# A transformer block on one core: another order of all its steps

## The chip, the cores and the metric

The kernel runs on one core of a Trainium2 chip. The core has TensorE (PE, with its weight loads shown apart as PEld), VectorE (DVE), ScalarE (ACT), GpSimd (POOL) and SyncE (SP), which here does nothing but issue transfers. Each engine takes its instructions from a queue of its own and in that queue's order; between queues, semaphores say when the data of one instruction are there for another. The metric is the device time of one execution in microseconds (us). Lower is better.

## The reference

2048 tokens of width 512 pass a normalized sliding-window attention (32 heads of 16, a window of 256) and a normalized gated feed-forward layer of width 1376, each with its input added:

```
q, k, v = qkv of layernorm(x) @ wqkv                 # 32 heads of 16
scores = einsum("bhqd,bhkd->bhqk", q, k) * (Dh ** -0.5)
mask = (idx[:, None] - idx[None, :] >= 0) & (idx[:, None] - idx[None, :] < W)   # W = 256
p = _softmax(where(mask, scores, -1e9))
h = x + (p @ v, heads put together) @ wo
g = layernorm(h) @ w_gate;  u = layernorm(h) @ w_up
out = h + (_sigmoid(g) * u) @ w_down
```

All inputs and the output are float32.

## The kernel before

**Numbers.** Every float32 product is made of float16 ones. A matrix is scaled by a power of two and split into a high half and a low half (a cast or copy, L355 and L357, then a subtraction, L362), and a product is three matmuls, high by high, high by low and low by high (L402 in `mm3`, also L1140 and L1317).

**Stage one, attention.** The tokens lie in 16 row tiles of 128, two to a block of 256 queries (8 blocks). For a block the steps are: load x (`load_x`, L473), layer norm (`normal`, L556 to L573: statistics on DVE, the root on POOL, the normalization), split, transposition on PE (L609) or by a transfer (L616); q and k (`do_qk`, L402, low half L661), v (`do_v`); keys and queries restacked through transfers (`do_keys`, L670 to L677, into `SK`; `do_queries`, L686, into `SQ`). `SK` has room for five half blocks, so a load into it waits until the scores that read its old content are done. Scores are computed twice: `do_s` (PE L740) for the row maxima, which DVE takes with the mask added (L725); `do_m` turns the maxima into two more rows of `SQ` (transposed by a transfer, L752, L756); `do_st` computes the transposed scores (L794 to L805), ACT their exponentials (L770), POOL cuts off what is masked (L778, L783). `do_pv` multiplies with v (L831), `do_o` transposes by a transfer and adds the halves into `OS` (L854, L861), and `do_wo` divides by the sums (L873, L875), splits, transposes, multiplies with wo (L402) and adds x (L899), which `load_again` (L480) has fetched a second time. Ahead of everything `prep` finds the largest element of wq, wk, wv and wo (L367 on ACT or L369 on DVE, the pieces together in L531), makes a scale of it (PE L380, DVE L384 to L388) and splits the weights (L537, L539).

Beside it, the weights of stage two are prepared: `do_amax` loads each piece of w_gate, w_up and w_down (L926) for its largest element (L369), `do_split` and `do_weights` load the pieces again and make scaled halves of them and of their sums.

**Stage two, feed-forward.** The row tiles go in 8 pairs, the columns in 3 cuts (512, 512, 352). `do_ln2` normalizes, splits and transposes a pair; `do_pair` makes the products of gate and up together with seven matmul groups where eight would be usual (a 2 x 2 scheme of Strassen's kind, L1140). Each group writes a PSUM bank; the result is copied out (`copied`, by L355 on ACT, by L357 or L359 on DVE) or added to what is there (`added`, L1161, L1163). A later group that adds onto the same bank waits for the copy. Then come sigmoid (ACT L1206), the product with up (DVE L1210), sums for the same scheme (L1224), halves, and a transposition by a transfer (`row`, L1240); `do_down` multiplies with w_down (L1317, L1323), adds into the rows (`taken`, `high`, L1288, L1300) and stores them (L1294).

**What sets the order.** Every step is a generator that stops once for each piece of work and says on which engines this piece may run. A table, `ORDER`, holds 4663 numbers, one for each piece of work, in the order in which all of them are recorded. `Planner.run` does no planning; it walks the table:

```
for code in ORDER:
    self.now = self.roots[code >> 7]
    item = self.now[code >> 2 & 31]
    costs, needs, *more = item[1]
    self.on = next(iter(costs)) if len(costs) == 1 else ENGINES[1 + (code & 3)]
```

The upper bits name the step (or the family of steps under one root), the middle bits the one of that family, and the last two bits the engine, DVE, ACT, POOL or DMA, where a piece can run on several. Since the program is recorded as it stands (`tc.manual_schedule`), the table fixes the order in each engine's queue and in SP's queue of transfers; waits come from the data and from the buffers' rings.

Of the kernel before, what the change touches and what calls it, by code (L numbers as in the profile page):

```python
# [61 lines left out]
    3203, 3331, 771, 899, 1027, 1155, 7424, 2179, 2435, 7808, 7426, 1411, 7424, 641, 2051, 7810, 7424, 641, 1539, 7424, 1667, 7808, 641, 7427, 7808,  # L62
    3459, 7810, 1795, 641, 2307, 6658, 640, 7424, 3587, 643, 7811, 640, 2691, 3075, 641, 7808, 2947, 640, 641, 2819, 640, 641, 8323, 640, 641, 8323,
    640, 8323, 1280, 1281, 1921, 8323, 1921, 3715, 8195, 1281, 1280, 1920, 8323, 13056, 1921, 8323, 8323, 8323, 1280, 12672, 13058, 1283, 8321, 8195,
    8195, 1280, 8195, 3843, 12674, 8195, 2561, 8195, 1920, 7042, 8320, 8195, 8195, 1281, 1923, 8193, 1280, 8451, 2561, 2560, 8192, 1281, 1280, 1281,
    8579, 9219, 1280, 1281, 2561, 3971, 8451, 9219, 1280, 8451, 8835, 12672, 8579, 6018, 1920, 8835, 12673, 8451, 13056, 9219, 1921, 8451, 12672,
    8451, 4099, 1921, 8451, 18304, 8451, 8963, 8579, 1922, 8449, 8579, 8963, 2560, 8579, 1921, 8448, 8579, 8835, 6274, 8579, 1921, 13056, 8579, 8963,
    17920, 12675, 13058, 8577, 2563, 12673, 8576, 17922, 1920, 1921, 8707, 13059, 18306, 7683, 8707, 1920, 13057, 1920, 7683, 1921, 8067, 1920, 8067,
    1920, 7683, 17920, 49667, 8067, 23168, 17921, 4227, 8067, 17920, 8707, 7683, 50691, 8064, 7681, 51075, 2560, 9091, 17923, 18304, 13443, 8707,
    2561, 13443, 23552, 13443, 2561, 13443, 17921, 13443, 18304, 4355, 23554, 13443, 18304, 13443, 6402, 9091, 13443, 28416, 13571, 13441, 13571,  # L70
    6530, 9091, 13571, 10371, 10371, 13571, 10372, 10376, 6786, 13571, 13440, 13571, 13571, 13571, 10371, 10371, 10371, 13569, 10384, 23170, 13699,
    10388, 13699, 50688, 2562, 13699, 10380, 49665, 13699, 13568, 13699, 13699, 13699, 13699, 23168, 10371, 10371, 14467, 10371, 13697, 13827, 10392,
    10400, 13827, 4483, 9347, 10396, 13827, 9348, 14211, 13827, 13696, 9347, 9347, 9347, 13827, 14083, 9352, 13827, 9360, 10883, 14211, 9356, 13827,
    10884, 13827, 28800, 14211, 18307, 13825, 10883, 9347, 10883, 18305, 9364, 10888, 13824, 9347, 10883, 2561, 9368, 18691, 13955, 10892, 33664,
    18691, 2561, 14083, 9347, 18691, 23169, 18691, 14467, 9372, 9347, 18691, 10896, 23170, 13955, 18819, 9376, 9603, 18691, 14467, 9604, 10883, 10883,
    9603, 10900, 18691, 10904, 51203, 9608, 18691, 23552, 10883, 9603, 9603, 18689, 18819, 10908, 4611, 9616, 18819, 10883, 9612, 18819, 10912, 18819,
    18688, 18819, 18819, 13955, 9603, 9603, 18819, 9603, 50435, 2560, 2561, 18817, 18947, 51331, 18947, 9620, 9624, 14339, 18947, 9628, 51073, 18947,
    18816, 14083, 9603, 18947, 2561, 18947, 14339, 18947, 2562, 18947, 50179, 9632, 11139, 10115, 19075, 18945, 10116, 10115, 11140, 19075, 10120,
    13955, 2561, 6146, 11139, 11139, 19075, 11144, 11148, 19075, 2561, 18944, 11139, 7170, 10115, 19075, 10115, 11152, 19075, 10128, 19075, 14339,
    10124, 11139, 12931, 11156, 34048, 28418, 11139, 10115, 10115, 19075, 12931, 19073, 10136, 11160, 12931, 10132, 51201, 19072, 11139, 11139, 10115,  # L80
    12931, 11164, 11168, 10140, 10115, 13315, 12929, 10144, 50433, 12416, 11651, 11651, 11651, 13315, 11652, 11656, 12419, 11660, 11651, 13315, 11664,
    11907, 11907, 13315, 11908, 11912, 0, 11651, 11651, 11651, 18563, 13313, 11668, 11672, 12419, 11676, 51329, 11651, 11907, 11907, 11680, 23171,
    11916, 18563, 49411, 11920, 23169, 23552, 19203, 11907, 11907, 11907, 18563, 11928, 23554, 19203, 11924, 11932, 11907, 16387, 16387, 11936, 9475,
    9475, 18563, 33666, 16388, 9477, 9481, 16392, 16387, 28802, 16387, 18561, 9475, 16396, 16387, 9475, 6914, 9485, 12544, 16387, 9489, 23555, 16400,
    12547, 16404, 9475, 23553, 16387, 18179, 16408, 28416, 16387, 9497, 15619, 16412, 9475, 4739, 18179, 16416, 50177, 50051, 15620, 15619, 9731,
    24195, 9501, 12547, 15624, 15619, 15619, 24195, 9733, 15628, 28417, 15619, 9731, 15632, 9731, 24195, 19203, 9741, 15636, 15619, 24195, 9737,
    15640, 15619, 15619, 9731, 15644, 9731, 9745, 24195, 15648, 9753, 15363, 9750, 9731, 15364, 15363, 24195, 9757, 19331, 9506, 15368, 10243, 16899,
    15363, 24195, 10245, 16900, 9494, 10243, 10243, 15372, 9859, 16899, 10249, 16899, 9762, 24195, 10253, 38912, 50049, 15363, 10243, 28418, 10243,
    9859, 10257, 16908, 10265, 16904, 7298, 49409, 15376, 16899, 28800, 10243, 15363, 16912, 16899, 10269, 10499, 4867, 18179, 15380, 50819, 9857,
    16916, 10499, 10274, 15363, 18179, 19331, 10501, 15384, 10505, 9856, 10499, 15363, 18177, 16899, 14851, 10499, 15388, 10509, 24323, 28419, 10513,  # L90
    16920, 10499, 14852, 10518, 15363, 10499, 10521, 16899, 15392, 24323, 10262, 50563, 16924, 10525, 14851, 16899, 24323, 14856, 19331, 50817, 14851,
    11011, 16928, 10530, 24323, 19459, 11013, 14851, 14860, 24323, 39296, 11011, 10627, 14851, 19459, 11011, 14851, 10627, 11021, 28801, 49795, 14872,
    19459, 11017, 14864, 28802, 24193, 14868, 11011, 9987, 11011, 11025, 14851, 24192, 24323, 11033, 2562, 11011, 14876, 14851, 14595, 11037, 28803,
    11267, 14880, 24323, 14595, 11030, 14596, 11269, 11267, 14595, 10625, 14600, 11267, 24323, 34050, 11273, 14604, 14595, 14595, 11277, 11042, 14608,
# [184 lines left out]
    61571, 62116, 61571, 62112, 62119, 61571, 61584, 61872, 61571, 62120, 62124, 60955, 61571, 62132, 61571, 62128, 61883, 62136, 61571, 62136, 61588,  # L279
    61571, 60315, 61571, 62139, 61571, 61571, 61592, 61888, 62211, 61888, 61884, 62211, 61891, 62211, 62211, 62212, 61884, 62211, 62140, 62211, 61887,  # L280
    62211, 62216, 62144, 62211, 62140, 62144, 62211, 62143, 62211, 62220, 62211, 61595, 62211, 62147, 62211, 62211, 62211, 59671, 62211, 60311, 62211,
    61591, 62224, 62211, 62211, 62211, 62211, 62228, 62211, 62231, 62211, 62211, 62211, 62232, 62235,
]

class Port(float):
# [1214 lines left out]
```

## Time and profile before

| | |
|---|---|
| median of 3 runs | 771.59 us (770.92 to 772.53) |
| the profiled execution | 770.99 us |
| its span on the core | 769.3 us |
| its mean granted TensorE clock | 0.989 |
| instructions | 19057 |
| transfers in the span | 118.57 MB, 154 GB/s |

A row of a timeline reads: start, duration, engine, source line, operation, result and source with their shapes, and in square brackets how long the engine had been idle and what ended that. `SPq` is SP's queue; its duration is that of issuing. `A <- B` among the waits means that an instruction of A's line waited and that B ended the wait. In a row of busy times "(x66)" is the number of instructions.

### The profile page before, as it was taken

The numbers are of one execution on the slowest core, as the hardware profiler recorded it, in microseconds if no ns is written. First come the engines' busy times: TensorE is split into PE (matmuls) and PEld (weight loads), VectorE is DVE, ScalarE is ACT, GpSimd is POOL, SyncE is SP. The second block draws the span as 40 slices with busy tenths as digits, with TensorE's granted clock in tenths as the row PEclk, the third lists the DMA queues.
The fourth block names the chain that finished last, engine by engine and source line by source line (L and its number), as shares of the span: only waits on it lengthen the run. The fifth ranks groups of instructions, "written<-read, shape, count | busy, mean of one in ns | idle before, by whom it ended". The sixth has DMA issues, their size and how long they took to land.

```text
span 769.3 us, 19057 instructions
## 1 busy us (share of the span) xinstructions
PE 729.6 (95%) x7030; PEld 502.0 (65%) x7030; DVE 692.9 (90%) x2067; ACT 436.9 (57%) x774; POOL 256.7 (33%) x319
## 2 busy tenths in 40 slices
PE   4899999999999999999999898699999999999997
PEld 3586678777686687686666554367565666666476
DVE  8999999978899999999998579999998989989973
ACT  5755788878688888798877667653222111121210
POOL 3333445535545466554757442240000000000000
PEclk9999999999999999999999999899999999999999
DMA  8586593886747989569587879455375665736535
GB/s 300 156 221 168 142 180 80 152 198 144 165 95 172 205 211 182 166 156 245 150 162 180 211 187 274 117 119 105 79 136 95 117 131 106 150 66 109 96 83 155
DMA packets 210318, 118.57 MB, mean 154 GB/s; under 512 B 174576, under 2 KB 183792, under 8 KB 210224
## 3 DMA queue, kind: packets, MB, share of 16 engines
q1 hardware_dynamic: 210224, 117.35, 67.9%
q8 instruction: 55, 0.90, 0.5%
q14 instruction: 39, 0.32, 0.2%
HBM read 43.65 MB, written 19.40 MB: 82 GB/s over the span
## 4 chain that ended last, share of the span: by engine, by line
PE 75%; DVE 11%; DMA 5%; issue 5%; ACT 3%; SPq 0%; DVEq 0%; ACTq 0%
PE mmp L402 18%; PE sp L1140 14%; PE mmp L1317 11%; PE pvp L831 7%; PE sp L740 6%; PE stp L1140 6%; PE pvp L1140 3%; PE stp L805 2%; PE stp L795 2%; DVE junk L725 2%; PE stp L794 1%; PE mmp L1323 1%; PE stp L796 1%; DMA oT<-whl 1%; ACT pa L770 1%
## 5 line engine op out<-in xcount | busy, mean ns | idle before, releaser
L725 DVE CUSTOM_DVE_ANT_0 junk<-sp,mask 128x320 uint8<-128x320 f32 (+4 forms) x512 | 215.4, 465 | 16.6 <-PE sp L740 14.0
L770 ACT ACTIVATE pa<-stp,kappa 128x512 f32<-128x512 f32 (+1 forms) x256 | 157.3, 645 | 48.0 <-PE stp L796 44.5
L1140 PEld LDWEIGHTS <-x 128*128 128x128 f16 x1008 | 98.3, 98 | 94.6 <-issue 10.1
L740 PE MATMUL sp<-SK,SQ 96*128 96x256 f16 (+3 forms) x960 | 129.6, 233 | 6.3 <-DVE mq L725 3.1
L402 PE MATMUL mmp<-xT,W 128*128 128x256 f16 x768 | 114.3, 281 | 3.3 <-DVE sq L661 1.7
L740 PEld LDWEIGHTS <-SQ 96*128 96x128 f16 x960 | 80.5, 97 | 30.9 <-issue 12.8
L1140 PE MATMUL sp<-W,x 128*128 128x512 f16 (+1 forms) x420 | 90.1, 351 | 6.5 <-ACT SQ L355 5.8
L770 ACT ACTIVATE pb<-stp,kappa 128x512 f32<-128x512 f32 x128 | 84.6, 685 | 19.7 <-PE stp L805 15.9
L402 PEld LDWEIGHTS <-W 128*128 128x128 f16 x768 | 71.4, 100 | 16.1 <-DVE W L539 2.9
L778 POOL TENSOR_SCALAR_AFFINE_SELECT pa<-pa 128x1024 f32<-128x1024 f32 x56 | 62.9, 1127 | 53.9 <-ACT pa L770 50.3
L831 PE MATMUL pvp<-pa,VT 128*17 128x128 f32 (+1 forms) x1408 | 62.5, 307 | 0.0
L795 PE MATMUL stp<-SQ,SK 100*128 100x256 f16 x224 | 60.2, 272 | 0.0
L563 POOL TENSOR_TENSOR rs<-rs,nhalf 128x1 f32<-128x1 f32 x32 | 20.2, 634 | 118.2 <-DVE rs L560 105.0
L783 POOL TENSOR_SCALAR_AFFINE_SELECT pa<-pa 128x512 f32<-128x512 f32 x64 | 42.6, 669 | 45.3 <-ACT pa L770 45.0
L1206 ACT ACTIVATE SQ<-sp,cg 128x512 f32<-128x512 f32 (+1 forms) x22 | 14.0, 636 | 76.6 <-PE sp L1140 76.3
L796 PE MATMUL stp<-SQ,SK 100*128 100x128 f16 x256 | 55.5, 219 | 0.7 <-ACT pb L770 0.4
L783 POOL TENSOR_SCALAR_AFFINE_SELECT pb<-pb 128x512 f32<-128x512 f32 x64 | 42.0, 658 | 42.6 <-ACT pb L770 40.1
L402 PE MATMUL mmp<-WO,oT 128*128 128x512 f16 x192 | 51.4, 389 | 2.5 <-DMA oT<-whl 2.5
L831 PEld LDWEIGHTS pvp<-pa,VT 128*17 128x17 f32 x1408 | 37.8, 97 | 22.7 <-issue 2.7
L362 DVE TENSOR_TENSOR SQ<-SQ,SQ 128x512 f16<-128x512 f32 (+3 forms) x93 | 50.2, 555 | 1.9 <-ACT SQ L355 1.3
L794 PE MATMUL stp<-SQ,SK 100*128 100x128 f16 x224 | 49.5, 221 | 1.3 <-DMA SQ<-mt 0.3
L805 PE MATMUL stp<-SQ,SK 100*128 100x256 f16 x256 | 48.1, 272 | 2.5 <-ACT pa L770 2.1
(226 smaller groups left out, 1445.8 us busy)
## 6 DMA issues: line engine op xcount, KB each, us to landing
SQ<-sq SPq DMA_DIRECT2D x96, 128.0 KB
wr<-chunk SPq DMA_DIRECT2D x28, 256.0 KB
SK<-mem SPq DMA_DIRECT2D x16, 384.0 KB
chunk<-in_wd_dram SPq DMA_DIRECT2D x20, 256.0 KB
X<-in_x_dram SPq DMA_DIRECT2D x16, 256.0 KB
mem<-sk SPq DMA_DIRECT2D x8, 512.0 KB
out_dram<-X SPq DMA_DIRECT2D x16, 256.0 KB
W<-wr SPq DMA_DIRECT2D x7, 512.0 KB
```

The lines of the kernel that those rows point to most:

```text
L402: PE.matmul(ps, a_of(a, k), b_of(b, k), start=(k == 0 and i == 0), stop=(k == n - 1 and i == 2))
L725: V.tensor_tensor_reduce(out=junk[:, c0:], in0=ps[:, c0:], in1=mask[:, c0:], scale=1.0, scalar=-3.0e38, op0=ALU.add, op1=ALU.max, accum_ou ...
L740: PE.matmul(ps[:, col:col + k1 - k0], q, SK[0:96, (2 * a + hf) % 5, 4 * (p % 2) + j, k0:k1], start=True, stop=True)
L770: S.activation(dst, a, AF.Exp, scale=kappa)
L778: G.affine_select(out=f, in_=f, pattern=[[0, 8], [-1, 128]], compare_op=ALU.is_gt, fill=0.0, base=0, channel_multiplier=1)
L783: G.affine_select(out=p, in_=p, pattern=[[0, 4], [1, 128]], compare_op=ALU.is_ge, fill=0.0, base=0, channel_multiplier=-1)
L795: PE.matmul(a[:, 128:384], ks(k0 + 1, g, j), qs(b, g, j, 0, 256), start=True, stop=True)
L796: PE.matmul(a[:, 384:512], ks(k0 + 3, g, j), qs(b, g, j, 128, 256), start=True, stop=True)
L805: PE.matmul(a[:, u, :], ks(k0 + 2, g, j + u), qs(b, g, j + u, 0, 256), start=True, stop=True)
L831: PE.matmul(ps[32 * j:32 * j + 17, u, q0:q1], VT[:, kt % 6, 8 * j + g, :], w[:, j, c:c + q1 - q0], start=first, stop=last, skip_group_chec ...
L1140: PE.matmul(ps, X2[p % 2][part][:, (a * COUNT[part] + at) * 2 + k, :], operand(c, j)[:, b, k, :], start=first and k == 0 and i == 0, stop= ...
L1317: PE.matmul(ps, hT[p, c, r][:, a, half * kinds[c] + i, :], W["d"][2 * c + i][:, b, j, :], start=fresh and c == 0 and i == 0 and n == 0, st ...
```

## The change

Only the table `ORDER` differs. Both tables have the same 4663 pieces of work. 109 of them run on another engine than before (57 leave DVE for ACT or POOL, 52 come to DVE), and the rest stand at other places. The start of the difference:

```
 ORDER = [
-    3203, 3331, 771, 899, 1027, 1155, 7424, 2179, 2435, 7808, 7426, 1411, 7424, 641, 2051, 7810, 7424, 641, 1539, 7424, 1667, 7808, 641, 7427, 7808,
...
+    3331, 899, 3203, 771, 1027, 1155, 7808, 3587, 2179, 7424, 2691, 2051, 7426, 641, 1539, 7810, 7424, 641, 2435, 7424, 7424, 641, 1795, 7808, 7427,
...
```

The first place is SP's queue at the start of the program, from its first transfer on; `X` holds the row tiles of x, `wq`, `wk`, `wv` and `OS` receive pieces of the weights:

```order
-L473 DMA X<-in_x_dram 128x512 x2
-L487 DMA wq<-in_wqkv_dram 128x512 x4
-L487 DMA wv<-in_wqkv_dram 128x512 x2
+L473 DMA X<-in_x_dram 128x512
+L487 DMA wq<-in_wqkv_dram 128x512
+L473 DMA X<-in_x_dram 128x512
+L487 DMA wq<-in_wqkv_dram 128x512 x3
+L473 DMA X<-in_x_dram 128x512
+L487 DMA wv<-in_wqkv_dram 128x512
+L487 DMA OS<-in_wo_dram 128x512
+L487 DMA wv<-in_wqkv_dram 128x512
```

Before, row tiles 0 and 1 came first and then the four pieces of wq. Now tile 1 comes first (3331), then a piece of wq (899), then tile 0 (3203), and the other three pieces; on DVE the statistics of tile 1 accordingly precede those of tile 0, while tile 0 is still normalized first.

The second place is SP's queue around the load of `SK` with the first half of block 4's keys. In the old order, from the transposition of a block's attention output (`oT<-whl`) to that load:

```order
L616 DMA_TRANSPOSE oT<-whl 128x8x128
L686 DMA SQ_73<-sq_102 32x2048 x2
L926 DMA chunk<-in_wd_dram 128x512
L756 DMA SQ_79<-mt 2x32x64 x2
L686 DMA SQ_73<-sq_102 32x2048
L926 DMA chunk<-in_wu_dram 128x512
L686 DMA SQ_73<-sq_102 32x2048
L926 DMA chunk<-in_wd_dram 128x512
L677 DMA SK<-mem 96x2048
```

In the new order:

```order
L616 DMA_TRANSPOSE oT<-whl 128x8x128
L854 DMA_TRANSPOSE RT<-RH 128x8x128
L686 DMA SQ_73<-sq_102 32x2048 x2
L926 DMA chunk<-in_wu_dram 128x512
L926 DMA chunk<-in_wd_dram 128x512
L677 DMA SK<-mem 96x2048
```

Two query loads and the maxima's transfer (L756) now stand ahead of the transposition, one of the loads of w_down pieces (L926) stands behind the keys, and a load of x by L480, which came after them, stands 31 places further ahead.

The third place is DVE's queue in stage two, at the last cut of pair 2 (`SQ<-sp` and `SQ<-stp` of 352 columns are copies of PSUM products). In the old order both copies were ACT's, and DVE had:

```order
L1288 SCALAR_TENSOR_TENSOR X<-mmp,cd,X 128x512
L1210 TENSOR_TENSOR SQ_73<-SQ_73 128x352
L1288 SCALAR_TENSOR_TENSOR X<-mmp,cd,X 128x512
L556 BN_STATS st_9054<-X 128x6
L558 BN_AGGR mv<-st_9054 128x2
L560 TENSOR_SCALAR rs<-mv 128x1
L1210 TENSOR_TENSOR SQ_73<-SQ_73 128x352
```

In the new order:

```order
L1288 SCALAR_TENSOR_TENSOR X<-mmp,cd,X 128x512
L1163 SCALAR_TENSOR_TENSOR SQ_73<-stp,SQ_73 128x352
L1210 TENSOR_TENSOR SQ_73<-SQ_73 128x352 x2
L357 COPY SQ_73<-sp 128x352
L357 CAST SQ_79<-SQ_73 128x352
L359 TENSOR_SCALAR SQ_73<-stp 128x352
L556 BN_STATS st_9070<-X 128x6
```

The two copies came to DVE, behind both multiplications of L1210 and ahead of the statistics of the next pair.

Elsewhere: in the attention stage between 160 and 417 us of the profile before, 22 pieces of work leave DVE and 17 come to it. Of the steps that leave, 5 are additions into `OS` (L861), 4 maxima (L369), 4 low halves (L362), 4 casts (L357), 3 copies of PSUM results and 2 sums of a pair (L1122); those that come are 6 additions, 2 maxima, 2 low halves, 4 casts, a PSUM copy and 2 multiplications of L875. In stage two 6 copies of PSUM products (`copied`) go from ACT to DVE and 5 the other way (with 2 more at 421 and 445 us, still in attention). At the end, the halves of the last transposed rows (L357, L362) stand ahead of two additions on DVE (L1288, L1300) that came before them, and on SP two stores (L1294) in place of one stand ahead of the last transposition (L1240).

442 rows, old and new, of the table ORDER are left out of this document.

## The prediction

> **What bounds the kernel now.** I read the page's totals and its chain first, then TensorE's waits, then busy times by stage.
>
> ```profile
> PE 729.6 (95%) x7030; PEld 502.0 (65%) x7030; DVE 692.9 (90%) x2067; ACT 436.9 (57%) x774; POOL 256.7 (33%) x319
> PE 75%; DVE 11%; DMA 5%; issue 5%; ACT 3%; SPq 0%; DVEq 0%; ACTq 0%
> ```
>
> TensorE is busy for 729.6 of 769.3 us and carries three quarters of the chain. A new order removes no matmul, so it can only win idle time of TensorE, 39.7 us, and stretches where a "busy" TensorE is fed slowly. VectorE, at 90%, is the second limit. TensorE's waits name what ended its idle time (columns: us in total, times, the longest):
>
> ```profile
> PE mmp L609 <- DVE RT L357: 7.0, 1, 7.0
> PE sp L1140 <- ACT SQ L355: 6.4, 2, 5.8
> PE sp L740 <- DVE mq L725: 3.1, 6, 1.2
> PE mmp L402 <- DMA oT<-whl: 2.5, 2, 2.1
> PE stp L805 <- ACT pa L770: 2.1, 2, 1.9
> PE sp L740 <- DMA SK<-mem: 1.6, 1, 1.6
> ```
>
> The reader is to see few, single waits: 7.0 before the first transposes, 5.8 once in the passage to the second stage, and 1.6 to 2.1 for a transfer here and there. Which stage lives under which limit, the windows tell (columns: stretch, its length, busy us of PE, PEld, DVE, ACT, POOL, granted clock, DMA share, GB/s):
>
> ```profile
> 200.00:220.00 20.00, 18.32 (x213) 14.02 (x210) 16.40 (x65) 13.74 (x22) 7.70 (x11) 0.91 0.62 144
> 400.00:420.00 20.00, 19.15 (x246) 12.74 (x245) 19.07 (x64) 14.58 (x25) 16.22 (x21) 1.00 0.79 192
> 480.00:500.00 20.00, 12.74 (x66) 6.85 (x65) 19.97 (x39) 13.25 (x26) 3.96 (x4) 0.83 0.50 113
> 520.00:740.00 220.00, 220.00 (x1428) 139.31 (x1426) 201.91 (x451) 45.92 (x83) 9.55 (x14) 1.00 0.57 108
> ```
>
> In attention (400 to 420) TensorE and VectorE are both near full. From 480 to 500 VectorE has no idle time and TensorE stands. From 520 to 740 TensorE has no idle time at all, so there the change can only lose.
>
> **The change, part by part.** The table holds the same 4663 steps, of which 109 change engine; TensorE's own order hardly moves. I go through the span and charge each part against the profiled execution's 770.99 us, its 769.3 of span and 1.7 around it. That execution is 0.6 below the median of the runs shown (771.59).
>
> *Start.* The first row tile of x is now loaded third, behind the second tile and a piece of wq. What hangs on it:
>
> ```profile
> 6.45 0.63 ACT L367 ACTIVATE W<-wq 128x512 f16<-128x512 f32 x1 [4.37 <-DMA wq<-in_wqkv_dram]
> 3.75 0.69 DVE L556 BATCH_NORM_STATS2 st<-X 128x6 f32<-128x512 f32 x1
> 4.77 0.68 DVE L556 BATCH_NORM_STATS2 st<-X 128x6 f32<-128x512 f32 x1
> 4.94 0.55 POOL L563 TENSOR_TENSOR rs<-rs,nhalf 128x1 f32<-128x1 f32 x1 [1.22 <-DVE rs L560]
> 5.91 0.54 DVE L573 TENSOR_SCALAR chunk<-X,mv,rs 128x512 f32<-128x512 f32 x1
> 8.13 0.43 DVE L357 CAST RT<-chunk 128x512 f16<-128x512 f32 x1
> 9.60 0.16 DVE L531 TENSOR_REDUCE am<-am 128x1 f32<-128x4 f32 x1 [1.05 <-ACT W L367]
> 12.38 0.61 PE L402 MATMUL mmp<-xT,W 128*128 128x256 f16 x2 [0.85 <-ACT W L537]
> ```
>
> ScalarE's first maximum waits for the third load, so the third place lands at 6.45; the first had landed by 3.75. From the statistics of the first tile to its root on POOL takes 5.49 - 3.75 = 1.74, and from the normalization (5.91) through split and second tile to the last cast 8.56 - 5.91 = 2.65. In the new order VectorE takes the second tile's statistics first, then the first's: 6.45 + 1.74 + 2.65 = 10.84. Behind stands the maximum of wq (L531), which came at 9.60 and was covered by 1.05 of idle time; it slips by 1.2. The scales, the weight pieces and the first matmul follow it without a gap, VectorE's queue stays full behind them, and nothing later catches up unless a stage has room. **+1.2**; ends: nothing, if x in third place lands as it did in second (statistics of the second tile started at 4.8 without a wait), and 1.3.
>
> *Keys of block 4, first half.* On SyncE's queue several loads stood ahead of the load of SK; one of them goes behind it, and a load of x goes far ahead.
>
> ```profile
> 198.58 2.21 SPq L926 DMA_DIRECT2D chunk<-in_wd_dram  x1
> 202.87 0.38 PE L805 MATMUL stp<-SQ,SK 100*128 100x256 f16 x2
> 204.49 6.62 DMA SK<-mem
> 211.16 0.47 PE L740 MATMUL sp<-SK,SQ 96*128 96x64 f16 x5 [1.58 <-DMA SK<-mem]
> ```
>
> The load overwrites keys that the scores of block 2 read last, which end at 202.87 + 0.38 = 203.25. It cannot be issued before that, so at most 204.49 - 203.25 = 1.2 of TensorE's 1.58 can be won, and something on the queue will take part of it: **-0.9** (0 to -1.6, the whole wait). The wait has a second price:
>
> ```profile
> 212.00:214.00 2.00, 2.00 (x16) 1.63 (x16) 1.99 (x9) 1.57 (x3) 0.00 (x0) 0.62 0.83 236
> 214.00:216.00 2.00, 2.00 (x16) 1.62 (x15) 1.00 (x4) 1.06 (x2) 0.00 (x0) 0.53 0.29 106
> 430.00:432.00 2.00, 0.47 (x3) 0.10 (x1) 0.70 (x2) 1.36 (x3) 0.00 (x0) 1.00 1.39 115
> ```
>
> Behind it TensorE's clock is 0.62 and 0.53 for two windows of 2 us: 0.38 x 2 + 0.47 x 2 = 1.7 us of matmul time lost, with VectorE idle for half of the second. A wait of 1.9 near 430 had no such sequel, so it doesn't come for certain; a shorter wait may escape it. I take half, **-0.8** (0 to -1.7). [...]
>
> *VectorE in attention, 160 to 417.* By the order, 22 steps leave VectorE for ScalarE or POOL there and 17 come to it. Their prices (columns: times; shortest, median, longest ns; first and last start):
>
> ```profile
> L861 DVE TENSOR_TENSOR OS<-RT x17: 429/436/869, 126.0 to 460.8; 128x272 f32<-128x272 f16 x17
> L369 DVE TENSOR_REDUCE amd<-chunk x7: 673/680/686, 196.1 to 247.2; 128x1 f32<-128x512 f32 x6, 96x1 f32<-96x512 f32 x1
> L362 DVE TENSOR_TENSOR whl<-OS,whl x9: 627/681/1218, 133.6 to 474.9; 128x512 f16<-128x512 f32 x9
> L357 DVE CAST whl<-OS x6: 415/420/806, 133.1 to 424.0; 128x512 f16<-128x512 f32 x6
> L875 DVE TENSOR_TENSOR OS<-OS,rc x7: 678/685/693, 132.4 to 463.7; 128x512 f32<-128x512 f32 x7
> L357 DVE COPY SQ<-sp x18: 515/681/693, 421.4 to 736.2; 128x512 f32<-128x512 f32 x13, 128x352 f32<-128x352 f32 x5
> ```
>
> Leaving: 5 adds (L861), 2 subtractions priced like them, 4 casts, and 4 maxima, 4 low halves and 3 PSUM copies at 0.68: 7 x 0.44 + 4 x 0.42 + 11 x 0.68 = 12.2. Coming: 6 adds, 4 casts, and 2 maxima, 2 low halves, 2 multiplies and 1 copy at 0.68: 6 x 0.44 + 4 x 0.42 + 7 x 0.68 = 9.1. Net 3.1 less. If TensorE were fed by VectorE alone, all of it would be won; if TensorE were the bound, nothing. In 400:420 both are within 1 us of full, so I take half: **-1.5** (0 to -3.1). What covers the steps that leave is ScalarE, 14.6 of 20, and POOL, 16.2 of 20.
>
> *Passage to the second stage, 420 to 505.* The waits on the transposes near 430 and 462 keep the same instructions ahead of them on ScalarE and SyncE: 0, though the first may now draw a slow clock, up to +1.7. In the VectorE-bound stretch up to 494, whose end releases TensorE's 5.8, two steps go and two come, each 0.4 to 0.7 by the rows above: **+0.2** (-0.6 to +0.6).
>
> *Feed-forward stage.* Six copies of PSUM products (L357, L359) go from ScalarE to VectorE, and five the other way. ScalarE had idle time; VectorE has a queue. One place, pair 2, last cut:
>
> ```profile
> 529.49 0.46 ACT L355 ACTIVATE SQ<-sp 128x352 f32<-128x352 f32 x1 [1.00 <-PE sp L1140]
> 529.12 0.74 DVE L1288 SCALAR_TENSOR_TENSOR X<-mmp,cd,X 128x512 f32<-128x512 f32 x1
> 530.78 0.52 DVE L1210 TENSOR_TENSOR SQ<-SQ 128x352 f32<-128x352 f32 x1
> 531.08 1.06 PE L1140 MATMUL sp<-W,x 128*128 128x352 f16 x6
> ```
>
> The copy ended at 529.95, and the product that adds onto the same bank starts at 531.08: 1.13 of room. Now the copy stands behind the add of L1288 and the multiply that came at 530.78: 529.86 + 0.52 + 0.51 (the shortest of its kind above) = 530.9, 0.2 in time. TensorE never waits as long as such margins hold. A loss at one or two of the six: **+0.5** (0 to +4.1, six times 0.68).
>
> *End.* TensorE waits 0.8 for the last transpose, which SyncE issues at 758.25, 11 us from the end. Its data are ready up to 1 us sooner, since two adds now stand behind them on VectorE, but two stores instead of one stand ahead of it on the queue:
>
> ```profile
> 757.59 0.57 SPq L1294 DMA_DIRECT2D out_dram<-X  x1
> 758.25 2.52 SPq L1240 DMA_TRANSPOSE RH<-SQ  x1
> 762.27 0.50 PE L1317 MATMUL mmp<-WD,RH 128*128 128x256 f16 x3 [0.81 <-DMA RH<-SQ]
> ```
>
> The second costs 0.6, so **-0.2** (0 to -0.8) is left.
>
> The sum is 1.2 - 0.9 - 0.8 - 1.5 + 0.2 + 0.5 - 0.2 = -1.5: 769.5 for the profiled execution, and 770.1 against the median.
>
> **The rivals.** *More of a gain.* x in third place lands early enough (by about 5.2) to leave the start as it is, and VectorE is the true bound through attention, so that all 3.1 arrive: 0 - 1.7 - 3.1 + 0.5 = -4.3, or 767.3. For it speaks VectorE's 19.07 of 20; against it, that TensorE shows only 3.1 us of waits for the row maxima (L725), and the landing at 6.45.
>
> *Slower, through the PSUM copies.* The mechanism is the one above: a copy that waits in VectorE's queue holds back the next product, in a stage where TensorE has no slack to give it back. It decides where VectorE's queue ahead of the copy exceeds the room (0.2 in the place worked out). If all six lose a copy's length, 4.1 stand in place of 0.5: 773.7, and 774 to 776 if one of the waits also slows the clock. For it: 201.91 of 220 busy on VectorE. Against it: the copies that went to ScalarE ease VectorE elsewhere, and the margin, though thin, is positive.
>
> *Nothing that counts.* TensorE's order is nearly the old one and its streams are full, so engines off its path may be shuffled without effect: 771.6.
>
> **How the numbers follow.** The forecast 770.1 has 0.45, the larger gain 0.20, the copies 0.28, no effect 0.07. What can be told from no change is about 0.2%, 1.5 us. The forecast's own range is 767.5 to 773; it lies on the edge of what can be told, so I give 0.22 of its chance to faster, 0.20 to the same and 0.03 to slower. With the others: faster 0.22 + 0.20 = 0.42, the same 0.20 + 0.07 = 0.27, slower 0.03 + 0.28 = 0.31. The range for 8 times in 10 reaches below the larger gain and past most of the copies' case: 766.0 to 775.5.
>
> **What would show it.** The start is right if L531 on VectorE starts near 10.8 and the first matmul of L402 moves from 12.4 to about 13.6. The keys' term is right if TensorE's wait for SK shrinks below 1 us and no window behind it has a clock near 0.6. The relief is right if VectorE is busy about 3 us less between 160 and 417 and the last row max of block 7 comes earlier by more than the start lost. The rival with the copies shows as waits of L1140 for L357 or L359 between 520 and 740, where TensorE has none now. The forecast is wrong if a new wait of over 1 us, with a slow clock behind it, stands anywhere between 160 and 505: one such costs up to 3.4 and eats the sum.

## The result and the profile after

The new order is slower: 776.13 us median (774.69 to 778.38, 7 runs) against 770.92 of the old order's runs beside it (766.17 to 772.53). The ratio is 1.0094, with a 95% interval of 1.0073 to 1.0116. That is under one per cent, and clear of the noise. A second set of runs of the same kernel gave 1.0095 (1.0075 to 1.0114). The forecast was 770.1, and its range ended at 775.5. The profiled execution took 777.85, its span 776.1.

The busy times of the page after (us, share of the span, instructions):

```profile
PE 731.5 (94%) x7030; PEld 503.2 (65%) x7030; DVE 695.1 (90%) x2061; ACT 438.9 (57%) x782; POOL 257.3 (33%) x322
```

VectorE was to lose 3 us of work in attention alone. It has six instructions fewer than before, yet is busy 2.2 us longer (692.9 before). Its instructions have become longer, not more. TensorE's waits after, the longest sums first:

```profile
PE mmp L609 <- DVE RT L357: 8.6, 1, 8.6
PE sp L1140 <- ACT SQ L355: 5.3, 2, 5.2
PE sp L740 <- DVE mq L725: 5.0, 6, 1.5
PE mmp L402 <- DVE sq L661: 3.2, 4, 1.8
...
PE mmp L402 <- ACT VT L355: 0.8, 2, 0.7
...
PE stp L1140 <- DVE SQ L359: 0.7, 1, 0.7
```

The wait for SK is gone; waits for VectorE's row maxima (3.1 before, 5.0 now) and others for VectorE have grown. Stretches of the same times as before, with 40 to 60 added (the work in them is not the same to the microsecond, since the new execution lags):

```profile
40.00:60.00 20.00, 17.08 (x162) 14.22 (x160) 18.55 (x78) 10.29 (x18) 9.05 (x13) 1.00 0.92 224
200.00:220.00 20.00, 19.51 (x274) 14.39 (x272) 18.89 (x70) 15.35 (x28) 8.84 (x12) 1.00 0.80 154
520.00:740.00 220.00, 218.80 (x1424) 138.83 (x1422) 204.81 (x461) 44.52 (x78) 15.39 (x20) 1.00 0.55 105
```

and 40 to 60 before:

```profile
40.00:60.00 20.00, 19.48 (x186) 16.65 (x184) 19.32 (x85) 11.53 (x20) 7.07 (x7) 1.00 0.84 215
```

There TensorE works 2.4 us less while POOL works 2.0 more. Taking each matmul after against the same matmul before, the median delay is 0.7 us for those at 20 to 40, 3.8 at 40 to 60 and 5.2 at 60 to 80. Most of the loss is there after 80 of 776 us. The delay falls to 3.2 at 80 to 100, where the old execution loses time of its own (at 76 and 88, see below), and is 4.9 at 100 to 120, 5.0 at 160 to 180, 2.7 at 220 to 240 (behind the old execution's wait for SK), 7.6 at 420 to 440, 7.8 at 600, and 6.8 at the end. What happens in the first part shows in the timeline of POOL and VectorE:

```profile
35.77 0.95 POOL L505 MEMSET SK<- 32x1024 f32 x1
35.95 1.05 DVE L573 TENSOR_SCALAR xn<-X,mv,rs 128x512 f32<-128x512 f32 x1
...
41.20 1.31 DVE L573 TENSOR_SCALAR xn<-X,mv,rs 128x512 f32<-128x512 f32 x1 [0.78 <-POOL rs L563]
41.28 0.95 POOL L505 MEMSET SK<- 32x1024 f32 x1
...
48.23 1.80 POOL L516 MEMSET SQ<- 32x2048 f32 x1
48.31 0.35 DVE L725 CUSTOM_DVE_ANT_0 junk<-sp,mask 128x192 uint8<-128x192 f32 x1
48.59 1.72 DVE L573 TENSOR_SCALAR xn<-X,mv,rs 128x512 f32<-128x512 f32 x1
...
59.71 1.80 POOL L516 MEMSET SQ<- 32x2048 f32 x1
59.78 2.01 DVE L573 TENSOR_SCALAR xn<-X,mv,rs 128x512 f32<-128x512 f32 x1
...
105.05 1.80 POOL L516 MEMSET SQ<- 32x2048 f32 x1
105.47 1.42 DVE L747 TENSOR_SCALAR mh<-mq 128x32 f16<-128x32 f32 x1
```

L505 and L516 clear or fill parts of `SK` and `SQ` once, on POOL, some time ahead of their first use. L573 is the normalization, usually 0.54 us long, L747 a step on only 128 x 32 numbers, usually 0.18. Wherever one of them overlaps a fill or a clear here, it ends 0.04 to 0.3 us behind the other's end (48.23 + 1.80 = 50.03; 48.59 + 1.72 = 50.31). I say that it is held, and call the time above its usual length the hold. The row maximum at 48.31, which reads PSUM, runs through in 0.35 us, the mean of its 16 like it. Within 110 us the new order held five such steps (0.5, 0.8, 1.2, 1.5 and 1.2 us), the old order two (L747 at 76, 1.5 us, and L573 at 88, 1.0 us); a cast (L357, near 31 us) is held by some 0.7 in both. The summaries by form (shortest, median, longest ns) say the same, L747 and L573 before, L573 after:

```profile
L747 DVE TENSOR_SCALAR mh<-mq x16: 116/176/1636, 69.0 to 417.1; 128x32 f16<-128x32 f32 x16
L573 DVE TENSOR_SCALAR xn<-X,mv,rs x12: 447/542/1521, 36.0 to 277.6; 128x512 f32<-128x512 f32 x12
```

```profile
L573 DVE TENSOR_SCALAR xn<-X,mv,rs x12: 535/546/2008, 35.9 to 282.3; 128x512 f32<-128x512 f32 x12
```

As far as these rows bear it out, the reading that the experiments test is this: a normalization, a step like L747 or a cast on VectorE stands still while a fill or a clear runs on POOL. The expectations put it wider, as theory A and later as the lock theory. The traces show the overlap and the length of the hold; what in the chip makes it is not shown. In one row the order is the other way round: at 41.20 the record has the normalization start 0.08 us ahead of the fill, and it ends 0.28 us behind that fill's end all the same (42.51 and 42.23).

Two more things stand beside the holds. The row at 41.20 says that VectorE was idle for 0.78 us ahead of it: the root that it needs (L563, at 40.61) stood in POOL's queue behind a fill (39.57). And behind the fifth hold the granted clock is low, in the second profile of the new order too (0.50 in the same window), though TensorE's longest single wait there is 0.65 us:

```profile
112.00:114.00 2.00, 2.00 (x15) 1.55 (x14) 1.87 (x9) 1.67 (x4) 1.93 (x4) 0.50 0.44 164
```

As a yardstick I add up, over all VectorE instructions, what each took above the lower quartile of its kind (same line, operation, names and shape) where that is over 0.15 us, and call it held time. The sum does not say what held them:

| profile | held up to 130 us | 130 to 420 | from 420 |
|---|---|---|---|
| before | 3.6 | 5.2 | 2.8 |
| after | 6.4 | 6.7 | 5.9 |

### The profile page after: what moved, and what is told of

Read it like the earlier page. It is cut to its first block, busy times and chain, and to the rows that moved or that the text cites. A ratio compares the mean times of both kernels' runs of the same rounds, so it can differ in the third digit from the quotient of the medians.

```text
span 776.1 us, 19078 instructions
## 1 busy us (share of the span) xinstructions
PE 731.5 (94%) x7030; PEld 503.2 (65%) x7030; DVE 695.1 (90%) x2061; ACT 438.9 (57%) x782; POOL 257.3 (33%) x322
## 5 line engine op out<-in xcount | busy, mean ns | idle before, releaser
L725 DVE CUSTOM_DVE_ANT_0 junk<-sp,mask 128x320 uint8<-128x320 f32 (+3 forms) x512 | 214.4, 464 | 15.0 <-PE sp L740 12.2
L770 ACT ACTIVATE pa<-stp,kappa 128x512 f32<-128x512 f32 (+1 forms) x256 | 156.6, 646 | 46.3 <-PE stp L796 43.6
L1140 PEld LDWEIGHTS <-x 128*128 128x128 f16 x1008 | 98.5, 98 | 95.5 <-issue 10.7
L740 PE MATMUL sp<-SK,SQ 96*128 96x256 f16 (+3 forms) x960 | 132.0, 233 | 6.2 <-DVE mq L725 5.0
L402 PE MATMUL mmp<-xT,W 128*128 128x256 f16 x768 | 114.8, 281 | 6.1 <-DVE sq L661 3.2
L740 PEld LDWEIGHTS <-SQ 96*128 96x128 f16 x960 | 82.1, 98 | 29.7 <-issue 11.1
L1140 PE MATMUL sp<-W,x 128*128 128x512 f16 (+1 forms) x420 | 90.5, 354 | 7.4 <-ACT SQ L355 5.2
L770 ACT ACTIVATE pb<-stp,kappa 128x512 f32<-128x512 f32 x128 | 84.7, 686 | 21.4 <-PE stp L805 20.5
L402 PEld LDWEIGHTS <-W 128*128 128x128 f16 x768 | 71.1, 100 | 20.8 <-DVE sq L661 4.1
L778 POOL TENSOR_SCALAR_AFFINE_SELECT pa<-pa 128x1024 f32<-128x1024 f32 x56 | 62.1, 1110 | 56.2 <-ACT pa L770 56.2
L783 POOL TENSOR_SCALAR_AFFINE_SELECT pa<-pa 128x512 f32<-128x512 f32 x64 | 42.3, 663 | 55.7 <-ACT pa L770 54.7
L795 PE MATMUL stp<-SQ,SK 100*128 100x256 f16 x224 | 60.0, 272 | 0.0
L783 POOL TENSOR_SCALAR_AFFINE_SELECT pb<-pb 128x512 f32<-128x512 f32 x64 | 42.0, 659 | 35.5 <-ACT pb L770 32.1
L402 PE MATMUL mmp<-WO,oT 128*128 128x512 f16 x192 | 50.7, 383 | 3.0 <-DMA oT<-whl 2.4
L563 POOL TENSOR_TENSOR rs<-rs,nhalf 128x1 f32<-128x1 f32 x32 | 19.8, 620 | 96.9 <-DVE rs L560 96.0
L362 DVE TENSOR_TENSOR SQ<-SQ,SQ 128x512 f16<-128x512 f32 (+3 forms) x93 | 50.9, 556 | 0.8
L402 PE MATMUL mmp<-W,xT 128*128 128x512 f16 x192 | 49.6, 378 | 0.9 <-ACT VT L355 0.7
```

The lines of the kernel that those rows point to most:

```text
L362: (G if plan.on == POOL_ else V).tensor_tensor(out=out, in0=a, in1=b, op=ALU.subtract)
L402: PE.matmul(ps, a_of(a, k), b_of(b, k), start=(k == 0 and i == 0), stop=(k == n - 1 and i == 2))
L725: V.tensor_tensor_reduce(out=junk[:, c0:], in0=ps[:, c0:], in1=mask[:, c0:], scale=1.0, scalar=-3.0e38, op0=ALU.add, op1=ALU.max, accum_ou ...
L740: PE.matmul(ps[:, col:col + k1 - k0], q, SK[0:96, (2 * a + hf) % 5, 4 * (p % 2) + j, k0:k1], start=True, stop=True)
L770: S.activation(dst, a, AF.Exp, scale=kappa)
L778: G.affine_select(out=f, in_=f, pattern=[[0, 8], [-1, 128]], compare_op=ALU.is_gt, fill=0.0, base=0, channel_multiplier=1)
```

## The experiments

Each ratio is to runs of the old order beside it. Their medians differ from set to set (770.92 above, 766.95 for the first four kernels here, 767.90, 768.30 and 769.23 for the later ones), so it is the ratios that can be compared, and where an expectation names a time it is to be read against the old order's.

### Which part of the order

The first 420 pieces of the old table end at about 66 us. Here they are put in the new table's sequence and on its engines, and the rest is left in the old one, and the other way round. The edits are long lists of numbers; this is a sketch of them, in which p is one occurrence of a piece (four pieces of the first kernel and two of the second stand later than it says):

```
 first = the first 420 pieces of old
-ORDER = old
+ORDER = [p for p in new if p in first] + [p for p in old if p not in first]
```

> The first 420 pieces of work of the old table (about the first 66 us) in the new order and on the new engines, everything behind them in the old order. Theory A (VectorE is held up while POOL writes: the new order puts its normalizations, L573, beside POOL's memsets, L505 and L516, and the 4 to 5 us lost by 60 us stay lost): 774 to 776 us, with L573 of 1.3 to 2.0 us near 41, 49 and 60. Rival B (the start's delay is absorbed by the waits of the old order near 77, 210 and 430, and the loss is made later): 770 to 772 us.

Measured 777.73; ratio 1.0117 (1.0081 to 1.0152). The first 66 us alone cost as much as the whole change, and more than either theory gave (774 to 776 is 1.004 to 1.0066 of 770.92). Part of it is made by the joint: TensorE waits 2.52 us at 88 for an exponential, which neither whole order does.

```
-ORDER = new
+ORDER = [p for p in old if p in first] + [p for p in new if p not in first]
```

> The reverse: the first 66 us in the old order, everything behind in the new one. Theory A: about 4 us less than the new order, 771 to 773 us, with no L573 over 1 us before 66 us. Rival B: 775 to 777 us, as the new order.

Measured 769.95; ratio 1.0043 (1.0022 to 1.0064). That is 4 us less than the new order by ratio, as theory A had it, though the later 90% of the new order still cost 0.4%. This joint too has a wait of its own, 1.58 us at 73 for a copy of v, which neither whole order has there; with such costs the two ratios add up to more than 1.0095.

### Shorter clears

```
-        G.memset(SK[96:128, i].rearrange("r s t -> r (s t)").bitcast(F32), TWO)
+        for q in range(4):
+            G.memset(SK[96:128, i].rearrange("r s t -> r (s t)").bitcast(F32)[:, 256 * q:256 * q + 256], TWO)
...
-        G.memset(SQ[i][96:128, 8 * f:8 * f + 8].rearrange("r s i u t -> r (s i u t)").bitcast(F32), 0.0)
+        for q in range(8):
+            G.memset(SQ[i][96:128, 8 * f:8 * f + 8].rearrange("r s i u t -> r (s i u t)").bitcast(F32)[:, 256 * q:256 * q + 256], 0.0)
```

> The new order, but POOL's memsets of SK (L505, 0.95 us) and SQ (L516, 1.80 us) are cut into pieces of 256 columns, same order, same values. Theory A (a VectorE instruction that meets a POOL instruction waits until that one instruction ends): the normalizations near 41, 49 and 60 wait for one short piece each, under 0.9 us in all, and 2 to 3 us come back: 773 to 774.5 us. Rival C (the normalizations are long for another reason, such as transfers writing to the same memory or the length of the POOL work as a whole): they stay at 1.3 to 2.0 us and the time at 775.5 to 777 us.

Measured 772.38; ratio 1.0058 (1.0028 to 1.0088). The normalization that took 1.72 (its line is L575 in this kernel):

```profile
46.83 2.36 POOL L518 MEMSET SQ<- 32x256 f32 x8
46.91 0.35 DVE L727 CUSTOM_DVE_ANT_0 junk<-sp,mask 128x192 uint8<-128x192 f32 x1
47.19 0.74 DVE L575 TENSOR_SCALAR xn<-X,mv,rs 128x512 f32<-128x512 f32 x1
```

Between two pieces VectorE gets its turn, within 0.2 us. The eight pieces cost POOL 2.36 us instead of 1.80. What is held up to 130 us falls from 6.4 to 0.7, and about 40% of the loss in time goes with it, less than expected. The longer fills also keep the root of the normalization near 41 waiting in POOL's queue: VectorE is idle for it for 1.37 us, where it was 0.78.

### The load ahead of the keys

The old order, with one load of a w_down piece (52611, L926) moved behind the load of `SK` for block 4, and nothing else:

```
-    39298, 34816, 52611, 27680, 28163,
+    39298, 34816, 27680, 28163,
...
-    22557, 26627, 29699, 13187, 26912,
+    22557, 26627, 29699, 52611, 13187, 26912,
```

> The old order with one transfer moved: the load of the w_down piece (L926) that held SyncE's queue for 2.2 us at 198.6 stands behind the load of SK for block 4. If the wait for SK and the slow clock behind it cost what they showed: 2 to 3.3 us less than the old order. Rival: the load of SK then waits for the scores of block 2 or lands as late as before, 0 to 0.9 us less, and the slow clock stays.

Measured 766.11; ratio 0.9971 (0.9946 to 0.9996). That is 2.2 us less, in the range given for the wait and the slow clock, but the interval reaches from 0.3 to 4.1 and takes in most of the rival's range too. Whether the wait comes in every execution, the old order profiled again is to tell:

> The old order unchanged, for a second profile of it: 765 to 771 us. All theories agree; it shows how much of the old profile's waits (1.5 us of L747 near 76, the wait for SK near 210, 430 and 462) is there in every execution.

One execution, 767.35, with a span of 765.6. Its window at the same place:

```profile
200.00:220.00 20.00, 19.76 (x249) 15.68 (x245) 18.67 (x77) 16.04 (x27) 8.77 (x12) 1.00 0.68 149
```

TensorE is busy 19.76 of 20 where the first profile had 18.32. The wait for SK is 0.15 us instead of 1.58, and the clock stays at 1.00 where it was 0.62 and 0.53. So the same queue gives a long wait, a short one or none. Among the profiles of kernels that leave this place in the old order, e1_new_start has it at full length, with the clock at 1.00 behind it, and e14_start_clears_moved has 0.59:

```profile
218.87 0.47 PE L740 MATMUL sp<-SK,SQ 96*128 96x64 f16 x5 [1.71 <-DMA SK<-mem]
```

The others (e7_old_short_pool, e9_old_clears_moved, e12_old_clear_on_norm) have none. Nor do the two kernels with the load moved (this one and e13_old_clears_keys), and no profile of a kernel with the new order there has it. The slow clock behind the wait stands in the first profile alone.

### The change again, and all of POOL's longer work in pieces

> The new order once more, unchanged, beside the next three. All theories: 0.7 to 1.1% slower than the old order.

Measured 775.33; ratio 1.0095 (1.0075 to 1.0114). The result stands.

In the next two, POOL's longer instructions except L861 are cut into two to eight pieces, in the new and in the old order (the fills and clears as above, and L362, L778, L783, L875, L1122, L1224), for example:

```
-            G.affine_select(out=f, in_=f, pattern=[[0, 8], [-1, 128]], compare_op=ALU.is_gt, fill=0.0, base=0, channel_multiplier=1)
+            for q in range(0, 8, 2):
+                G.affine_select(out=f[:, q:q + 2], in_=f[:, q:q + 2], pattern=[[0, 2], [-1, 128]], compare_op=ALU.is_gt, fill=0.0, base=0, channel_multiplier=1)
```

> The new order with all of POOL's longer instructions in pieces: the memsets of L505 and L516, subtractions (L362), sums (L1122, L1224), the product of L875 in four, the masks of L778 and L783 in four and two; L861 stays whole. Theory A (VectorE waits for single POOL instructions, through the whole attention stage and the passage): VectorE's long instructions (L747 and L748 near 264, L1026 and L1045 near 290 to 326) come down below 0.6 us beyond their usual length, and the time falls further than with the memsets alone, to 0.0 to 0.4% above the old order. Rival D (only the memsets mattered; the rest of the loss comes from the new places in the queues): 0.5 to 0.7% above, as with the memsets alone. More pieces cost POOL some 0.06 us each; if POOL becomes late, it is slower than that.

> The old order with the same pieces. Theory A: its own 12 us of such waits on VectorE fall by half, but most of them lie where VectorE has room: 0.0 to 0.5% faster than the old order. Rival D: no change within 0.2%, or slower by what the pieces cost.

778.23, ratio 1.0132 (1.0112 to 1.0152), and 772.71, ratio 1.0056 (1.0040 to 1.0071): both worse. Cutting is not free. The groups of L778 by busy time, before, and where its line is L787 with four pieces in the old order (columns: busy us, mean ns | idle before):

```profile
L778 POOL TENSOR_SCALAR_AFFINE_SELECT pa<-pa 128x1024 f32<-128x1024 f32 x56 | 62.9, 1127 | 53.9 <-ACT pa L770 50.3 <-issue 3.5
```

```profile
L787 POOL TENSOR_SCALAR_AFFINE_SELECT pa<-pa 128x256 f32<-128x256 f32 x224 | 90.2, 433 | 21.5 <-ACT pa L778 18.8 <-issue 2.3
```

62.9 us become 90.2, on the path from the exponentials to the next matmul. That is slower than either theory's figure, though both expectations allowed for a cost of the pieces. The two kernels mix a cure with a cost and can't settle the question; moving the instructions without cutting them can.

### The same work of POOL at other places

The old order, with the two clears that meet L747 and L573 moved into idle time of POOL:

```
-    16387, 9475, 6914, 9485, 12544,
+    16387, 9475, 9485, 12544,
...
-    34048, 28418, 11139, 10115,
+    34048, 28418, 6914, 11139, 10115,
...
-    10265, 16904, 7298, 49409, 15376,
+    10265, 16904, 49409, 15376,
...
-    16928, 10530, 24323, 19459,
+    16928, 10530, 7298, 24323, 19459,
```

> The old order with two of POOL's four clears of SQ moved and nothing else: the one that ran at 76.6 us beside L747 goes into POOL's idle stretch behind 66.6, the one that ran at 87.9 beside L573 goes to 94.9. Lock theory (a VectorE instruction that needs both its operands from SBUF stands still while a POOL instruction runs): L747 falls from 1.64 to 0.18 us, L573 at 88 from 1.52 to 0.54, the sum of VectorE's excess from 11.4 to about 9; PE gains 1 to 2 us at these places and the time falls by 0.8 to 2 us (0.1 to 0.25%). Rival (the long instructions on VectorE wait for something else, and are hidden): both instructions stay long, or fall without the time following; ratio 1.000 within 0.1%.

Measured 765.55; ratio 0.9972 (0.9953 to 0.9992): faster than the old order. At these two places L747 is back at 0.18, L573 at 0.55.

The opposite: the old order with a third clear moved from 64.2, where it meets nothing, onto a normalization:

```
-    18944, 11139, 7170, 10115, 19075,
+    18944, 11139, 10115, 19075,
...
-    10896, 23170, 13955, 18819,
+    10896, 23170, 7170, 13955, 18819,
```

> The old order with one clear of SQ moved onto a norm step: from 64.2 us, where it meets nothing, to 56.0, where VectorE runs L573 at 56.4. Lock theory: this one L573 grows from 0.54 to 1.7 to 2 us, and PE is some 1 us later behind it; the time grows by 0.5 to 1.5 us (0.06 to 0.2%). Rival (a clear on POOL does not touch VectorE): L573 stays at 0.54, ratio 1.000 within 0.1%.

Measured 768.36; ratio 0.9999 (0.9982 to 1.0016). The timelines at this place, first of the kernel ahead, without the clear, and then of this one:

```profile
54.27 0.29 DVE L725 CUSTOM_DVE_ANT_0 junk<-sp,mask 128x128 uint8<-128x128 f32 x1
54.48 0.55 DVE L573 TENSOR_SCALAR xn<-X,mv,rs 128x512 f32<-128x512 f32 x1
54.94 0.35 DVE L725 CUSTOM_DVE_ANT_0 junk<-sp,mask 128x192 uint8<-128x192 f32 x1
```

```profile
54.32 1.80 POOL L516 MEMSET SQ<- 32x2048 f32 x1
54.51 0.28 DVE L725 CUSTOM_DVE_ANT_0 junk<-sp,mask 128x128 uint8<-128x128 f32 x1
54.72 1.68 DVE L573 TENSOR_SCALAR xn<-X,mv,rs 128x512 f32<-128x512 f32 x1
56.32 0.34 DVE L725 CUSTOM_DVE_ANT_0 junk<-sp,mask 128x192 uint8<-128x192 f32 x1
56.72 0.27 PE L740 MATMUL sp<-SK,SQ 96*128 96x256 f16 x1 [0.76 <-DVE mq L725]
```

The row maxima behind the normalization are late by its 1.13 us, and TensorE waits for them. Matmul for matmul this kernel runs behind the one ahead by 0.2 us up to 55, by 1.3 from 60 on, 2.7 from 80 on (behind L747, 1.64 long) and 3.7 from 90 on (behind L573, 1.52 long), and it keeps that distance up to 400. Three collisions hold VectorE for 1.13 + 1.46 + 0.97 = 3.6 us and TensorE loses 3.5: one for one. The two kernels differ in the places of three clears alone, so this pair isolates the holds. In time the two kernels lie 2.8 us apart (768.36 and 765.55). Against the old order the one added collision, some 1.1 us or 0.14%, can't be told from nothing by its interval; only the trace shows it.

The decisive one: the new order with its three fills and three of its clears moved into POOL's idle time behind 63 us, and nothing else changed:

```
-    8448, 8579, 6402, 8579, 1921,
+    8448, 8579, 8579, 1921,
...
-    1921, 8067, 6530, 17920, 8067,
+    1921, 8067, 17920, 8067,
...
-    8065, 8707, 6274, 18304, 17923,
+    8065, 8707, 18304, 17923,
...
-    10384, 13569, 6786, 13699, 10380,
+    10384, 13569, 13699, 10380,
...
-    18691, 10904, 6914, 23552, 9603,
+    18691, 10904, 23552, 9603,
...
-    18819, 28418, 9603, 9603,
+    18819, 28418, 6402, 6530, 6274, 6786, 6914, 7170, 9603, 9603,
...
-    14624, 17155, 7170, 11789, 11395,
+    14624, 17155, 11789, 11395,
```

> The new order with six POOL steps moved and nothing else: the three fills of SK at 30.9, 35.9 and 41.4 us and the three clears of SQ at 48.3, 59.8 and 105.2 go into POOL's idle stretch behind 63.4. No instruction is cut in pieces, POOL does the same work. Lock theory: the five long runs of L573 and L747 (1.05, 1.31, 1.72, 2.01, 1.42 us) fall to 0.54 and 0.18; the excess of VectorE falls from 18 to about 13 us; the time falls by 3 to 5 us against the new order, to a ratio of 1.003 to 1.006 to the old. Rival (what costs the time is the new order of PE's and VectorE's own steps in the first 66 us): the time stays, ratio 1.008 to 1.011.

Measured 768.93; ratio 1.0014 (0.9997 to 1.0030), better than the 1.003 to 1.006 expected. Six of POOL's 322 instructions at other places take away 0.8% of the 0.95%. Not all of that is holds: VectorE's idle 0.78 us ahead of the normalization at 41 and the low clock at 112 are gone as well (the low clock is not the hold's doing alone: e3_new_short_memsets has 0.50 at 108 to 110 without the hold). The page's busy times and the stretch from 40 to 60:

```profile
PE 730.2 (95%) x7030; PEld 502.4 (65%) x7030; DVE 687.5 (90%) x2061; ACT 438.2 (57%) x782; POOL 258.1 (34%) x322
```

```profile
40.00:60.00 20.00, 18.97 (x179) 16.04 (x177) 19.03 (x84) 11.33 (x20) 8.71 (x12) 1.00 0.94 233
```

The same 2061 instructions of VectorE take 687.5 us instead of 695.1, POOL's 322 take 258.1 instead of 257.3, and TensorE has 1.9 us of its 2.4 back. Its wait for the row maxima falls from 5.0 to 1.2:

```profile
PE sp L740 <- DVE mq L725: 1.2, 2, 0.9
```

### The start

As the last kernel, with x tile 0 loaded first again:

```
-    3331, 899, 3203, 771,
+    3203, 3331, 899, 771,
```

> As e10_new_clears_moved, with the load of x tile 0 in first place again instead of third. If the start term of the prediction (+1.2 us) is right, this is 0.5 to 1.5 us faster than e10_new_clears_moved. Rival: PE's first matmul waits for tile 1 and the identity anyway, and the time is that of e10_new_clears_moved within 0.3 us.

Measured 769.72; ratio 1.0017 (0.9999 to 1.0035), as good as 1.0014. The rival has the time right and the reason wrong: the first transposition does start 0.6 us sooner (8.00 instead of 8.59), but nothing of it is left at the end.

### What adds up, and the rest

> The old order with the two clears of e9_old_clears_moved and the load of e4_old_keys moved, nothing else. If the two gains are of different waits and add: ratio 0.994 to 0.996. Rival (the gain of e4_old_keys was chance, its interval ended at 0.9996): the ratio of e9_old_clears_moved, 0.996 to 0.998.

Both edits of the old order together, those of e9_old_clears_moved and e4_old_keys. Measured 765.10; ratio 0.9947 (0.9929 to 0.9964). It beats both whole orders, the old one by half a per cent. That the gains add is likely but not certain: this interval and that of e9_old_clears_moved (0.9953 to 0.9992) overlap. That the moved load gains its part by the wait for SK is not shown: neither of these two profiles has the wait.

> As e1_new_start (the first 420 steps in the new order, the rest in the old one), with the six POOL steps of e10_new_clears_moved moved behind the norm step's rs. Lock theory: the held instructions of the first 110 us fall away and with them 5 to 7 us of the 9: ratio 1.000 to 1.005. Rival (the joint of the two orders or PE's own order costs it): ratio above 1.008.

The kernel of e1_new_start with the six steps of e10_new_clears_moved moved. Measured 771.56; ratio 1.0040 (1.0020 to 1.0060), down from 1.0117. Most of what the new first 66 us cost is the place of POOL's steps there too. Of the 0.4% that stays, 2.6 us are the wait at the joint, for an exponential (L770), here at 82 us.

## Why the prediction was wrong, point by point

**The step that failed** is ahead of all terms: "109 change engine; TensorE's own order hardly moves". POOL's own steps are in no term of the sum. A step that keeps its engine and its length was put at nothing wherever it went, and VectorE's work was priced by the median of its kind. Six fills and clears of POOL, none of which changes engine or length, stand in the new order where they meet VectorE: four a normalization, one the small step L747, one a cast (as in the old order). They hold VectorE for 5.9 us in the profile after, and by the new order with them moved away they are worth some 6 us (1.0095 against 1.0014). The sign stood in rows that the prediction quoted for their medians: 429/436/869 for L861, 627/681/1218 for L362, 415/420/806 for a cast. A longest of twice the median, at one size, asks for a cause.

**The terms in the sum were wrong too.** The old order has two such holds of its own, worth some 2 us (0.9972). So what was left out is about 4 of the 7 us between the two orders. With both freed of these holds the new order is still slower, 768.93 against 765.55, and the intervals don't overlap (0.9997 to 1.0030 against 0.9953 to 0.9992): some 3 us, where the sum had -1.5. Where they lie is known in part only. Nor does TensorE's own order stay: by lines, names and shapes, the longest sequence that both profiles have in common is 6010 of 7030 matmuls. What that costs was not tried.

**Start, +1.2.** The mechanism is right. In the profile after, L531 came at 10.07, not 10.84, since tile 0 landed at 5.73 in third place, and the first matmul of L402 moved from 12.38 to 12.83:

```profile
5.73 0.69 DVE L556 BATCH_NORM_STATS2 st<-X 128x6 f32<-128x512 f32 x1 [1.10 <-DMA X<-in_x_dram]
10.07 0.15 DVE L531 TENSOR_REDUCE am<-am 128x1 f32<-128x4 f32 x1
12.83 0.61 PE L402 MATMUL mmp<-xT,W 128*128 128x256 f16 x2 [0.78 <-DVE xT L357]
```

But 12.38 is the latest of the old starts. Over all profiles this matmul comes at 11.03 to 12.38 with the old start (eight, median 11.46) and at 12.32 to 13.41 with the new one (seven, median 13.03): 1.6 us later, more than the term had. What is left of it at the end is open: e11_new_clears_x0 takes 0.6 of it back and is no faster.

**Keys, -0.9 and -0.8.** Both were read off one execution, and the size differs from one to the next: where the old order stands here, the wait is 1.58, 0.15, 1.71 and 0.59 us in four of seven profiles, and the slow clock stands behind it in one. In the new order the wait is gone, as forecast. By the two kernels with the load moved it may be worth some 2 us in the mean (0.9971, and 0.9947 against 0.9972), but neither shows that the gain is this wait. The term is not refuted; it was a mean taken from one case.

**VectorE in attention, -1.5.** The relief did not come. Between 160 and 417 on the clock VectorE is busy 2.4 us less (238.0 before, 235.6 after, 3.1 forecast), but the new execution lags, so that this is not the same work. From the same matmul to the same matmul (before, and after):

```profile
160.00:417.00 257.00, 251.84 (x3167) 185.18 (x3169) 237.99 (x843) 207.50 (x347) 143.94 (x174) 0.99 0.77 172
164.40:424.60 260.20, 252.75 (x3171) 186.07 (x3174) 237.50 (x841) 211.68 (x359) 140.06 (x171) 0.99 0.77 173
```

VectorE's work is the same to 0.5 us, and the stretch takes 3.2 us longer, although the old execution lost time at the keys in it; between the second profiles of the two orders it takes 3.5 longer. Even with the six steps moved, the same matmuls fall from 2.5 us behind those of e9_old_clears_moved at 140 to 5.4 at 380, and are 2.3 behind at 500. One place is a copy of v on ScalarE, for which TensorE now waits 0.69 at 165 (L402 for L355 above). The rest was not tried; what is held between 130 and 420 differs by 1 us between these two kernels (6.7 and 5.7) and explains only a part.

**Passage, +0.2.** The delay is 7.6 at 420 to 440 and 6.4 at 500 to 520, and 7.3 and 7.4 between the second profiles: near nothing, as forecast, with a spread of over 1 us.

**Feed-forward, +0.5.** The delay grows from 6.4 to 7.8 by 600, between the second profiles from 7.4 to 8.5: more than the forecast, inside its range. One place is the wait of L1140 for L359 above, 0.7 at 577.6, a copy on VectorE as the rival had it. It is late because the cast ahead of it meets a POOL instruction and takes 1.40 us instead of 0.43:

```profile
575.70 1.16 POOL L362 TENSOR_TENSOR SQ<-SQ,SQ 128x512 f16<-128x512 f32 x1 [2.18 <-ACT SQ L355]
575.73 1.40 DVE L357 CAST SQ<-SQ 128x512 f16<-128x512 f32 x1
```

In the second profile of the new order the cast runs first, and this wait is not there. So the rival's way of losing time came once, through a hold; its 4.1 did not come.

**End, -0.2.** The delay shrinks by 1.0 (0.5 between the second profiles). TensorE's wait of 0.81 for the last transposition is gone.

## What to carry to other kernels

When an order is changed, ask for every step that moves what runs beside it, also where its own engine has time to spare: in these traces a clear on an idle POOL was free where VectorE read PSUM (a row maximum took its usual 0.35 us) or had two operands in SBUF (a subtraction took its usual 0.69), and not where it normalized (1.68 instead of 0.55). Look at the longest of a group, not only at its median, before pricing by the median; profile the kernel before a second time before pricing a wait that stands there once; and compare busy times between the same instructions, not between the same times. Move such a step before cutting it up: moving cost nothing here (0.9972 in the old order, 1.0014 instead of 1.0095 in the new one), and cutting most of POOL's work cost the old order 0.6%.

## What the runs showed of the hardware

A small instruction was held as fully as a large one: the 128 x 32 step of L747 for 1.46 us, a 128 x 512 normalization for 0.5 to 1.5. Put for every VectorE instruction with its operands in SBUF, the theory is too wide. In the new order with six steps moved, a subtraction of two SBUF operands runs at its usual length (0.69 us, the mean of four like it in the same profile) in the midst of fills, which read nothing:

```profile
58.07 2.73 POOL L505 MEMSET SK<- 32x1024 f32 x3
60.18 0.69 DVE L362 TENSOR_TENSOR WO<-OS,WO 128x512 f16<-128x512 f32 x1
60.74 5.29 POOL L516 MEMSET SQ<- 32x2048 f32 x3
```

while in the changed kernel products of two SBUF operands and POOL's additions and subtractions, which read SBUF, each end behind the other in turns:

```profile
324.80 0.75 DVE L1026 SCALAR_TENSOR_TENSOR chunk<-X,sg,chunk 128x512 f16<-128x512 f32 x1
324.91 1.23 POOL L861 TENSOR_TENSOR OS<-RT 128x272 f32<-128x272 f16 x1
325.46 1.22 DVE L1045 SCALAR_TENSOR_TENSOR X<-X,ratio 128x512 f32<-128x512 f32 x1
326.09 1.57 POOL L362 TENSOR_TENSOR whl<-OS,whl 128x512 f16<-128x512 f32 x1
326.61 1.60 DVE L1026 SCALAR_TENSOR_TENSOR chunk<-X,su,chunk 128x512 f16<-128x512 f32 x1
```

L1026 takes 0.75 when it comes first and 1.60 when it comes second; L861, usually 0.73, takes 1.23, and POOL's L362, usually 1.13, takes 1.57. These rows differ in what the two instructions read; no run changed that alone. Where VectorE works 19 of 20 us ahead of TensorE (19.32 at 40 to 60 before), three holds passed on to TensorE in full (3.5 of 3.6 us). The profile counts them as busy time of VectorE (the same 2061 instructions took 695.1 us, and 687.5 with six steps moved), so no list of waits shows the holds themselves.
